# Attention with adaptive layer norm: transposing pairs of bfloat16 columns as one float32

## The chip, the core and the metric

The kernel runs on one core of a Trainium2 chip. A core has five engines that run their own instruction streams and wait for each other through semaphores: TensorE (matmuls, called PE in the profile, its weight loads PEld), VectorE (DVE), ScalarE (ACT), GpSimd (POOL) and SyncE (SP), which here only issues DMA transfers. [...] The metric is the device time of one execution in microseconds (us), lower is better.

## The reference

The program is one transformer block with conditioning. Cut to what matters:

```python
mod = (silu(c) @ w_mod).reshape(1, 6, 1, 640)          # sa, ca, ga, sb, cb, gb
h = layernorm(x) * (1 + ca) + sa                        # x: [1, 2048, 640]
q = (h @ wq) per head                                   # 32 heads, width 128
p = softmax(q @ k_cache.T * 128 ** -0.5)                # [32, 2048, 2048]
x = x + ga * ((p @ v_cache) @ wo)
h = layernorm(x) * (1 + cb) + sb
x = x + gb * B(h)                                       # token-mixing block and MLP, F = 1728
```

All inputs and the output are bfloat16. The keys and values of the 32 heads (2048 x 128 each) are inputs; the softmax runs over 2048 keys for each of 2048 queries.

## The kernel before

**Order of the work.** The kernel is written as one long list of operations; a small recorder (class `Prog`) appends each to its engine's stream in the order of the program, derives which other operations it depends on from the names of the buffers it reads (`r`) and writes (`w`), and emits semaphore waits for them. Nothing is reordered later, so the order in the code is the order on each engine. A transfer belongs to the stream of the engine that issues it; nearly all are issued by SyncE, one after the other.

**Stages.** A preamble loads x, normalizes it, transposes it into `hT` and computes the modulation rows. Then comes the attention loop (line 552), which takes most of the time, and last the output projection and block B.

**The attention loop.** One step `s` handles one tile of 128 queries of one head (`h, j = divmod(s, 16)`): 32 heads x 16 tiles = 512 steps, and 12 more to drain. In a step:

- `qk(s, half)`: TensorE computes the scores of the 128 queries against 2048 keys into the PSUM buffer `Sps`, in two halves of 1024 keys (two matmuls of 512 columns each). There is one `Sps`, so a half is free only when VectorE has read it.
- L594: VectorE reads each half, multiplies by -scale, writes it as float32 into `negS` (three buffers) and takes the minimum. L604: GpSimd combines the two halves' minima.
- L607: ScalarE computes the exponential of the 2048 columns into the bfloat16 tile `Pb` of a ring of `RP = 10` tiles.
- The tile has to be transposed so that keys lie on the partitions. This goes one of two ways. Most tiles go by DMA: `transpose(g, n)` (L231) has SyncE issue a transpose of one or two neighbouring tiles from `Pb` to `PTs`. The tiles named in `PE_STEPS` go over TensorE instead: tiles 3 and 10 of a head, and tiles 2, 3 and 10 in every fourth head (`h % 4 == 1`), 72 of 512 in all.
- `pv(g, half)` (L314), eight steps later (`PVD`): sixteen matmuls of the transposed tile, as weights, with `Vaug`, which holds V and a column of ones that yields the softmax's denominator. The result is accumulated in PSUM (`PO`), copied out by ScalarE every second step (L585), divided by GpSimd (L462) and written to DRAM (`o_scratch`).
- `q_piece` (L246) and `q_evac` (L253): the projection of the next head's queries is spread over the steps in 20 matmuls; ScalarE copies it out four times a head.

SyncE also issues, in each head, the transposing load of the next keys (L214, at j = 2), the load of wq (j = 6) and of V (j = 9).

**Transposes on TensorE.** `t_piece(g, r, q)` does a quarter of a tile: four 128x128 bfloat16 blocks, each loaded as weights and multiplied with the identity `ident` in transpose mode, into one of two PSUM banks (`JBb`, shared with the query projection). A tile takes two steps, named by the second numbers in `PE_STEPS`: r = 0 in the first, r = 1 in the second. After two pieces `t_evac(g, r)` copies 1024 bfloat16 columns from PSUM to the ring. ScalarE does it (L271, 104 times) except where `by_dve` holds (r = 1 of tiles 2 and 3), where VectorE does (L273, 40 times). In the stream, ScalarE's copies stand ahead of the step's exponential; VectorE's stand behind its two halves of the scores.

`PTs[:, b, kt, :]` is the block of key tile `kt` with the 128 queries side by side; PV reads it as weights without a step.

Of the kernel before, what the change touches and what calls it, by code (L numbers as in the profile page):

```python
# [8 lines left out]
BF16 = mybir.dt.bfloat16  # L9
# [114 lines left out]
def bass_adaLN_cond__mha_block_cached__mixer_s_mlp__prompt_kernel(  # L124
# [6 lines left out]
    KT = D // 128  # L131
# [14 lines left out]
    with ExitStack() as es:  # L146
# [3 lines left out]
        ident = sb("ident", [128, 128], BF16)  # L150
        mod_bc = sb("mod_bc", [128, 4 * D], F32)
# [6 lines left out]
        if True:  # L158
            with ExitStack() as es1:
# [6 lines left out]
                sb1("pad", [128, 32], F32)  # L166
# [4 lines left out]
                small = sb1("small", [128, 4 * NQT + 32], F32)  # L171
                hTx = sb1("hTx", [128, US], BF16)
                Of = sb1("Of", [128, 4, 2, 130], F32)
                On = sb1("On", [128, 2, 4, 128], BF16)
                mv = small[:, 0:2 * NQT].rearrange("p (t z) -> p t z", z=2)
# [12 lines left out]
                PTs = ring[:, RP:2 * RP].rearrange("p r (k q) -> p r k q", k=NKT)  # L188
                flat = ring[:].rearrange("p r s -> p (r s)")
# [16 lines left out]
                assert CO + 8 * KT <= 2 * RP * SK and XO + NQT * D <= WO_ and WO_ + KT * 2 * D <= 10 * SK  # L206
# [49 lines left out]
                def t_piece(g, r, q):  # L256
                    jb = bank(("t", g, r))

                    def f(t):
                        for z in range(4 * q, 4 * q + 4):  # L260
                            kt = 8 * r + z
                            ins = t.transpose(JBb[jb][:, z * 128:(z + 1) * 128], Pb[:, g % RP, kt * 128:(kt + 1) * 128], ident[:])
                        return ins
                    G.op("tensor", f, r=[("Pb", g % RP)], w=[("J", jb)])

                def t_evac(g, r):
                    jb = bank(("t", g, r))
                    dst = PTs[:, g % RP, r * 8:(r + 1) * 8, :]
                    src = JBb[jb].rearrange("p (k q) -> p k q", k=8)
                    if not by_dve(g, r):  # L270
                        G.op("scalar", lambda a: a.copy(dst, src), r=[("J", jb)], w=[("PT", g % RP, r)])  # L271
                    else:
                        G.op("vector", lambda v: v.tensor_copy(dst, src), r=[("J", jb)], w=[("PT", g % RP, r)])  # L273

                by_dve = lambda g, r: r == 1 and g % NQT in (2, 3)
# [31 lines left out]
                def pv(g, half):  # L307
                    hb = (g // NQT) % 2
                    b = g % RP
                    ob = PO[:, ((g // 2) % 2) * 512 + (g % 2) * 130:]  # L310

                    def f(t):
                        for kt in range(half * 8, half * 8 + 8):
                            ins = t.matmul(ob[:, 0:129], PTs[:, b, kt, :], Vaug[:, hb, kt, 0:129],  # L314
                                           start=(kt == 0), stop=(kt == NKT - 1))
                        return ins
                    G.op("tensor", f, r=[("PT", b, half), ("V", hb), "ones"], w=[("O", (g // 2) % 2)])
# [34 lines left out]
                G.op("gpsimd", lambda g: g.memset(ident[:], 0.0), w=["id0"])  # L352
                G.op("gpsimd", lambda g: g.memset(ones_f, 1.0), w=["onesf"])
                G.op("gpsimd", lambda g: g.affine_select(out=ident[:], in_=ident[:], pattern=[[-1, 128]],
                                                         compare_op=ALU.not_equal, fill=1.0, base=0, channel_multiplier=1),
                     r=["id0"], w=["ident"])
                G.op("gpsimd", lambda g: g.memset(Vaug[:, :, :, 128:130], 1.0), w=["ones"])
# [38 lines left out]
                def to_hT(cc):  # L396
                    for k in range(KT):
                        b = (4, 5, 3, 4, 5)[k % 5] if cc == NQC - 1 else (cc * KT + k) % 6

                        def f(t, k=k, b=b):  # L400
                            for z in range(4):
                                ins = t.transpose(TB[b][:, z * 128:(z + 1) * 128], x_sb[:, 4 * cc + z, k * 128:(k + 1) * 128], ident[:])
                            return ins
                        G.op("tensor", f, r=["ident"] + [("xh", 4 * cc + z) for z in range(4)] + XK[cc], w=[TK[b]])
# [147 lines left out]
                for s in range(NG + PVD + LAG):  # L552
# [35 lines left out]
                    for fn, x, y in evacs:  # L588
                        if fn is q_evac or not by_dve(x, y):
                            fn(x, y)  # L590
                    for half in range(2):
                        if s < NG:
                            r8 = s % 8
                            G.op("vector", lambda v, half=half, s=s, r8=r8: v.tensor_scalar(  # L594
                                out=negS[:, s % 3, half * 1024:(half + 1) * 1024],
                                in0=Sps[:, half * 1024:(half + 1) * 1024],
                                scalar1=-SCALE, scalar2=None, op0=ALU.mult, op1=ALU.min,
                                accum_out=(nm0 if half == 0 else nm1)[:, r8:r8 + 1]),
                                r=[("S", half)], w=[("negS", s % 3), ("nmh", half, r8)])
                    for fn, x, y in evacs:  # L600
                        if fn is t_evac and by_dve(x, y):
                            fn(x, y)
# [307 lines left out]
```

## Time and profile before

| | |
|---|---|
| Time, median of 3 runs | 1569.87 us (1567.64 to 1571.41) |
| Profiled execution, span from first to last instruction | 1568.9 us (this one has no time recorded beside its span) |
| Attention loop, first to last L594 | 35.4 to 1251.8 us |
| TensorE / VectorE / ScalarE / GpSimd busy | 1472.3 / 1398.3 / 1275.9 / 623.0 us |
| L594, VectorE, 1024 times | 1177.7 us, mean of one 1224 ns |
| L607, ScalarE, 512 times | 1045.7 us, mean of one 2066 ns |
| L262, TensorE transposes, 1152 times | 218 ns each, overlapping |
| L271 ScalarE copies, 104; L273 VectorE copies, 40 | 1.06 and 0.69 us each |
| L231, transposes by DMA, 248 issues | median 4.34 us on SyncE's queue, 7.1 us to landing |
| TensorE clock granted | 0.998 of full |

How to read the profile: a line of the groups gives the source line, the engine, the operation, output <- input, shapes and count; then busy time, mean of one, and the time its engine stood idle just ahead of it with what ended that idle time. A timeline row is start, length, engine, line and operation; `x2` means that two neighbours were merged. Lengths of neighbours on one engine overlap, so what an instruction costs its engine is the distance to the next start. In the lines of waits the three numbers are total us, times and the longest.

### The profile page before, as it was taken

The page shows a single profiled execution, that of the slowest core. Times are in us where ns is not written, and L with a number is a line of the kernel's source. Part 1 is how long each engine was busy: PE and PEld are TensorE (multiplying, and loading weights), DVE is VectorE, ACT ScalarE, POOL GpSimd, SP SyncE. Part 2 cuts the span into 40 slices and gives each one's busy share as a digit, 9 for nine tenths or more (in the row PEclk, how much of TensorE's full clock was granted, in tenths as well). Part 3 has the DMA queues.
Part 4 walks back from the last instruction along what each step waited for, and adds up shares of the span by engine and source line. Part 5 has one row for each costly group of instructions (what it writes and reads, how often), then busy time and mean ns, then how long its engine had stood idle before and what let it go on. Part 6 is the DMA issues. An engine that isn't in the chain of part 4 may idle for free.

```text
span 1568.9 us, 33553 instructions
## 1 busy us (share of the span) xinstructions
PE 1472.3 (94%) x13947; PEld 923.4 (59%) x13175; DVE 1398.3 (89%) x2471; ACT 1275.9 (81%) x1121; POOL 623.0 (40%) x1396
## 2 busy tenths in 40 slices
PE   5899999999999999999999999999999899999999
PEld 3466666666665566566656666566566655554545
DVE  6999999999999999999999999999999937667435
ACT  4999999999999999999999999999999900034230
POOL 0144444444444444444444444444444433323100
PEclk9999999999999999999999999999999999999999
DMA  9999999999999999999999999999999999725100
GB/s 298 239 221 239 237 242 237 233 241 243 237 240 233 239 232 232 240 236 235 229 237 236 233 243 249 226 242 243 235 241 237 238 246 190 157 53 144 38 22 34
DMA packets 1172828, 334.59 MB, mean 213 GB/s; under 512 B 1153280, under 2 KB 1166656, under 8 KB 1172672
## 3 DMA queue, kind: packets, MB, share of 16 engines
q1 hardware_dynamic: 1164192, 311.30, 100.8%
q0 software_dynamic: 6144, 16.79, 3.5%
q10 hardware_dynamic: 2336, 4.34, 0.8%
q8 instruction: 108, 1.77, 0.5%
q14 instruction: 48, 0.39, 0.1%
HBM read 43.48 MB, written 19.40 MB: 40 GB/s over the span
## 4 chain that ended last, share of the span: by engine, by line
ACT 40%; DVE 23%; PE 19%; DMA 9%; issue 7%; POOL 1%; POOLq 0%; DVEq 0%
ACT ring L607 32%; DVE negS L594 20%; DMA ring<-ring 8%; PE Sps L540 8%; PE Sps L847 4%; ACT ring L271 3%; ACT kv L253 2%; ACT Of L585 2%; PE QPp L798 2%; PE Oaug L798 2%; DVE ring L273 1%; PE Sps L783 1%; DVE ring L379 1%; DMA negS<-o_scratch 1%; PE PTp L314 1%
## 5 line engine op out<-in xcount | busy, mean ns | idle before, releaser
L594 DVE TENSOR_SCALAR_CACHE_REDUCE negS<-Sps 128x1024 f32<-128x1024 f32 x1024 | 1177.7, 1224 | 19.4 <-PE Sps L15 18.5
L607 ACT ACTIVATE ring<-negS,small 128x2048 bf16<-128x2048 f32 x512 | 1045.7, 2066 | 13.7 <-POOL small L604 12.5
L314 PEld LDWEIGHTS PTp<-kv,ring 128*128 128x128 bf16 x8192 | 554.1, 98 | 325.0 <-issue 69.6
L314 PE MATMUL PTp<-kv,ring 128*128 128x129 bf16 x8192 | 645.3, 220 | 25.0 <-DMA ring<-ring 23.9
L15 PE MATMUL Sps<-kv 128*128 128x512 bf16 x1024 | 387.9, 379 | 16.8 <-DVE negS L594 9.9
L604 POOL TENSOR_SCALAR small<-small 128x1 f32<-128x1 f32 x512 | 146.4, 286 | 621.8 <-DVE negS L594 621.7
L301 PE MATMUL Sps<-kv 128*128 128x512 bf16 x919 | 354.3, 386 | 27.8 <-DVE negS L594 16.5
L462 POOL TENSOR_SCALAR On<-Of,small 128x128 bf16<-128x128 f32 x512 | 191.0, 373 | 13.0
L301 PEld LDWEIGHTS Sps<-kv 128*128 128x128 bf16 x1024 | 98.1, 96 | 141.7 <-DVE negS L594 121.6
L455 POOL TENSOR_TENSOR small<-Of,small 128x4 f32<-128x4 f32 x128 | 133.1, 1040 | 8.8 <-ACT Of L585 8.7
L469 POOL DMA_DIRECT2D o_scratch<-On x128 | 103.1, 806 | 40.8 <-POOL On L462 37.2
L585 ACT COPY Of<-PTp 128x259 f32<-128x259 f32 x256 | 108.6, 424 | 13.2 <-PE PTp L314 13.2
L246 PE MATMUL Oaug<-hTx,kv 128*128 128x512 bf16 x268 | 101.9, 385 | 3.7 <-DVE hTx L411 3.7
L246 PE MATMUL QPp<-hTx,kv 128*128 128x512 bf16 x259 | 97.7, 382 | 2.6 <-ACT hTx L406 2.1
L728 ACT ACT_TABLE_LOAD x1 | 1.3, 1283 | 112.6 <-POOL hTx L746 112.6
L594 DVE DVE_READ_ACCUMULATOR negS<-Sps 128x1 f32 x1024 | 90.3, 88 | 0.0
L271 ACT COPY ring<-Oaug 128x1024 bf16<-128x1024 bf16 x72 | 77.0, 1069 | 0.0
L641 POOL TENSOR_SCALAR negS<-negS 128x1 f32<-128x1 f32 x48 | 24.2, 504 | 125.2 <-DVE negS L650 125.2
L540 PE MATMUL Sps<-wo,negS 128*128 128x128 bf16 (+1 forms) x503 | 69.9, 298 | 1.2 <-DMA negS<-o_scratch 0.8
L540 PE MATMUL Sps<-wo,hTx 128*128 128x512 bf16 (+1 forms) x502 | 69.3, 297 | 0.5
L851 DVE TENSOR_TENSOR ring<-Sps,ring 128x640 f32<-128x640 f32 x15 | 12.4, 824 | 59.5 <-PE Sps L847 59.5
L655 DVE TENSOR_TENSOR ring<-Sps,mod_bc 128x640 f32<-128x640 f32 x16 | 13.1, 821 | 53.6 <-PE Sps L540 32.9
(88 smaller groups left out, 1052.7 us busy)
## 6 DMA issues: line engine op xcount, KB each, us to landing
kv<-in_A_v_cache_dram SPq DMA_DIRECT2D x32, 512.0 KB, 5.0
o_scratch<-On POOLq DMA_DIRECT2D x128, 128.0 KB, 4.7
kv<-in_A_wq_dram SPq DMA_DIRECT2D x32, 160.0 KB, 3.2
wo<-in_A_wo_dram SPq DMA_DIRECT2D x1, 5120.0 KB, 16.5
ring<-ring SPq DMA_TRANSPOSE x248, 7.1
ring<-in_A_x_dram SPq DMA_DIRECT2D x5, 640.0 KB, 6.6
ring<-in_w_mod_dram SPq DMA_DIRECT2D x1, 3200.0 KB, 13.8
out_dram<-wo SPq DMA_DIRECT2D x15, 160.0 KB, 1.8
```

Source lines behind the costliest of these rows:

```text
L15: return t.add_instruction(mybir.InstMatmult(name=t.bass.get_next_instruction_name(), ins=[t.lower_ap(rhs), t.lower_ap(lhsT)], outs=[t.low ...
L246: G.op("tensor", lambda t: t.matmul(JB[jb], wq[:, hb, q, :], hT[:, q, cc * 512:(cc + 1) * 512], start=(q == 0), stop=(q == KT - 1)), r=[(" ...
L271: G.op("scalar", lambda a: a.copy(dst, src), r=[("J", jb)], w=[("PT", g % RP, r)])
L301: ins = (t.matmul if c2 == 0 else partial(same_weights, t))(Sps[:, col:col + 512], QT[:, hb, j * 128:(j + 1) * 128], KTs[:, hb, col:col + ...
L314: ins = t.matmul(ob[:, 0:129], PTs[:, b, kt, :], Vaug[:, hb, kt, 0:129], start=(kt == 0), stop=(kt == NKT - 1))
L455: G.op("gpsimd", lambda g: g.tensor_tensor(out=rl[:, 4 * b:4 * b + 4], in0=Of[:].rearrange("p a z d -> p (a z) d")[:, 4 * b:4 * b + 4, 128 ...
L462: G.op("gpsimd", lambda g: g.tensor_scalar(out=On[:, b, z, :], in0=Of[:, 2 * b + z // 2, z % 2, 0:128], scalar1=rl[:, 4 * b + z:4 * b + z ...
L540: ins = t.matmul(YB[b][:, c0:c0 + cw], OTj[pr % 2][:, 2 * hh + z, :], wo[:, hh, c0:c0 + cw], start=(hh == 0), stop=(hh == H - 1))
L585: G.op("scalar", lambda a, p=p: a.copy(Of[:, p % 4].rearrange("p z d -> p (z d)")[:, 0:259], PO[:, (p % 2) * 512:(p % 2) * 512 + 259]), r= ...
L594: G.op("vector", lambda v, half=half, s=s, r8=r8: v.tensor_scalar(out=negS[:, s % 3, half * 1024:(half + 1) * 1024], in0=Sps[:, half * 102 ...
L604: G.op("gpsimd", lambda g, r8=r8: g.tensor_scalar(out=nm[:, r8:r8 + 1], in0=nm0[:, r8:r8 + 1], scalar1=nm1[:, r8:r8 + 1], scalar2=None, op ...
L607: G.op("scalar", lambda a, s=s, r8=r8: a.activation(Pb[:, s % RP, :], negS[:, s % 3, :], ACT.Exp, bias=nm[:, r8:r8 + 1], scale=-1.0), r=[( ...
```

## The change

The tiles that go over TensorE are moved as float32: two neighbouring bfloat16 columns count as one 4-byte element.

- `t_piece` reads `Pb` as 1024 float32 columns and does two 128x128 float32 transposes in a quarter where there were four bfloat16 ones, with a float32 identity `identf`. The PSUM bank then holds, for each of 128 pairs and each query, the pair.
- So that a pair holds the columns i and 128 + i of a block of 256 keys, VectorE writes `negS` interleaved for these tiles (`is_pe(s)`): the output pattern runs over 128 elements with a step of two float32. The exponential passes the order on.
- `t_evac` copies 512 float32 columns, always on ScalarE; `by_dve` is gone, and the copies that were behind VectorE's halves now stand ahead of the exponential on ScalarE.
- `pv` reads the weights of such a tile from `PTr` with a step of two bfloat16.
- The ones in `Vaug` are no longer a memset: GpSimd writes pairs (1, 0) into the ring, TensorE transposes them as float32, ScalarE copies them, and GpSimd writes `Vaug`'s ones from the result. `identf` is a GpSimd copy of `ident`.
- In SBUF `ident` moves into the ring's preamble part, `mod_bc` and `small` change places, `pad` goes. Which tiles go over TensorE and which by DMA (`PE_STEPS`, `is_pe`) is the same.

```diff
-        ident = sb("ident", [128, 128], BF16)
-        mod_bc = sb("mod_bc", [128, 4 * D], F32)
...
-                sb1("pad", [128, 32], F32)
+                small = sb1("small", [128, 4 * NQT + 32], F32)
...
-                small = sb1("small", [128, 4 * NQT + 32], F32)
+                mod_bc = sb1("mod_bc", [128, 4 * D], F32)
...
+                identf = sb1("identf", [128, 128], F32)
...
+                PTr = ring[:, RP:2 * RP].rearrange("p r (k q z) -> p r k q z", k=NKT // 2, z=2)
...
                 def t_piece(g, r, q):
                     jb = bank(("t", g, r))
+                    src = Pb[:, g % RP, :].bitcast(F32)
 
                     def f(t):
-                        for z in range(4 * q, 4 * q + 4):
-                            kt = 8 * r + z
-                            ins = t.transpose(JBb[jb][:, z * 128:(z + 1) * 128], Pb[:, g % RP, kt * 128:(kt + 1) * 128], ident[:])
+                        for z in range(2 * q, 2 * q + 2):
+                            c0 = (4 * r + z) * 128
+                            ins = t.transpose(JB[jb][:, z * 128:(z + 1) * 128], src[:, c0:c0 + 128], identf[:])
                         return ins
-                    G.op("tensor", f, r=[("Pb", g % RP)], w=[("J", jb)])
+                    G.op("tensor", f, r=[("Pb", g % RP), "identf"], w=[("J", jb)])
 
                 def t_evac(g, r):
                     jb = bank(("t", g, r))
-                    dst = PTs[:, g % RP, r * 8:(r + 1) * 8, :]
-                    src = JBb[jb].rearrange("p (k q) -> p k q", k=8)
-                    if not by_dve(g, r):
-                        G.op("scalar", lambda a: a.copy(dst, src), r=[("J", jb)], w=[("PT", g % RP, r)])
-                    else:
-                        G.op("vector", lambda v: v.tensor_copy(dst, src), r=[("J", jb)], w=[("PT", g % RP, r)])
-
-                by_dve = lambda g, r: r == 1 and g % NQT in (2, 3)
+                    dst = ring[:, RP + g % RP, r * 1024:(r + 1) * 1024].bitcast(F32)
+                    G.op("scalar", lambda a: a.copy(dst, JB[jb]), r=[("J", jb)], w=[("PT", g % RP, r)])
...
-                            ins = t.matmul(ob[:, 0:129], PTs[:, b, kt, :], Vaug[:, hb, kt, 0:129],
+                            pt = PTr[:, b, kt // 2, :, kt % 2] if is_pe(g) else PTs[:, b, kt, :]
+                            ins = t.matmul(ob[:, 0:129], pt, Vaug[:, hb, kt, 0:129],
...
-                G.op("gpsimd", lambda g: g.memset(Vaug[:, :, :, 128:130], 1.0), w=["ones"])
+                G.op("gpsimd", lambda g: g.tensor_copy(identf[:], ident), r=["ident"] + ringk(IO, IO + 128), w=["identf"])
+                half1 = flat[:, 0:256].rearrange("p (q z) -> p q z", z=2)
+                G.op("gpsimd", lambda g: g.memset(half1, 0.0), w=["h0", ("Pb", 0)])
+                G.op("gpsimd", lambda g: g.memset(half1[:, :, 0], 1.0), r=["h0"], w=["h1"])
+                G.op("tensor", lambda t: t.transpose(JB[0][:, 0:128], flat[:, 0:256].bitcast(F32), identf[:]),
+                     r=["h1", "identf"], w=[("J", 0)])
+                G.op("scalar", lambda a: a.copy(flat[:, 256:512].bitcast(F32), JB[0][:, 0:128]), r=[("J", 0)], w=["h2"])
+                G.op("gpsimd", lambda g: g.tensor_copy(
+                    Vaug[:, :, :, 128:130], flat[:, 256:384].rearrange("p (b k y z) -> p b k y z", b=2, k=NKT, z=2)[:, :, :, :, 0]),
+                    r=["h2", ("Pb", 0)], w=["ones"])
...
                     for fn, x, y in evacs:
-                        if fn is q_evac or not by_dve(x, y):
-                            fn(x, y)
+                        fn(x, y)
                     for half in range(2):
                         if s < NG:
                             r8 = s % 8
-                            G.op("vector", lambda v, half=half, s=s, r8=r8: v.tensor_scalar(
-                                out=negS[:, s % 3, half * 1024:(half + 1) * 1024],
-                                in0=Sps[:, half * 1024:(half + 1) * 1024],
-                                scalar1=-SCALE, scalar2=None, op0=ALU.mult, op1=ALU.min,
+                            dst = negS[:, s % 3, half * 1024:(half + 1) * 1024]
+                            src = Sps[:, half * 1024:(half + 1) * 1024]
+                            if is_pe(s):
+                                dst = dst.rearrange("p (b i z) -> p b z i", b=4, z=2)
+                                src = src.rearrange("p (b z i) -> p b z i", b=4, z=2)
+                            G.op("vector", lambda v, half=half, dst=dst, src=src, r8=r8: v.tensor_scalar(
+                                out=dst, in0=src, scalar1=-SCALE, scalar2=None, op0=ALU.mult, op1=ALU.min,
                                 accum_out=(nm0 if half == 0 else nm1)[:, r8:r8 + 1]),
                                 r=[("S", half)], w=[("negS", s % 3), ("nmh", half, r8)])
-                    for fn, x, y in evacs:
-                        if fn is t_evac and by_dve(x, y):
-                            fn(x, y)
```

More of the change, by code (lines that the diff above doesn't have):

```diff
@@ L205, in bass_adaLN_cond__mha_block_cached__mixer_s_mlp__prompt_kernel @@
                 s_col = flat[:, CO + 7 * KT:CO + 8 * KT]
-                assert CO + 8 * KT <= 2 * RP * SK and XO + NQT * D <= WO_ and WO_ + KT * 2 * D <= 10 * SK
+                IO = CO + 8 * KT
+                ident = flat[:, IO:IO + 128]
+                assert IO + 128 <= 2 * RP * SK and XO + NQT * D <= WO_ and WO_ + KT * 2 * D <= 10 * SK
                 PO = PTp[:].bitcast(F32)
@@ L350, in bass_adaLN_cond__mha_block_cached__mixer_s_mlp__prompt_kernel @@
                 G.dma("sync", lambda e: e.dma_start(wo[:], A_wo.rearrange("(h p) n -> p h n", p=128)), "wo", w=["wo", "woz", "wo4"])
-                G.op("gpsimd", lambda g: g.memset(ident[:], 0.0), w=["id0"])
+                G.op("gpsimd", lambda g: g.memset(ident, 0.0), w=["id0"])
                 G.op("gpsimd", lambda g: g.memset(ones_f, 1.0), w=["onesf"])
-                G.op("gpsimd", lambda g: g.affine_select(out=ident[:], in_=ident[:], pattern=[[-1, 128]],
+                G.op("gpsimd", lambda g: g.affine_select(out=ident, in_=ident, pattern=[[-1, 128]],
                                                          compare_op=ALU.not_equal, fill=1.0, base=0, channel_multiplier=1),
                      r=["id0"], w=["ident"])
-                G.op("gpsimd", lambda g: g.memset(Vaug[:, :, :, 128:130], 1.0), w=["ones"])
+                G.op("gpsimd", lambda g: g.tensor_copy(identf[:], ident), r=["ident"] + ringk(IO, IO + 128), w=["identf"])
[8 more added lines that the diff above has]
+                    r=["h2", ("Pb", 0)], w=["ones"])
                 G.op("scalar", lambda a: a.activation(s_col, c_sb, ACT.Silu), r=["c"], w=["scol"])
@@ L401, in f @@
                             for z in range(4):
-                                ins = t.transpose(TB[b][:, z * 128:(z + 1) * 128], x_sb[:, 4 * cc + z, k * 128:(k + 1) * 128], ident[:])
+                                ins = t.transpose(TB[b][:, z * 128:(z + 1) * 128], x_sb[:, 4 * cc + z, k * 128:(k + 1) * 128], ident)
                             return ins
-                        G.op("tensor", f, r=["ident"] + [("xh", 4 * cc + z) for z in range(4)] + XK[cc], w=[TK[b]])
+                        G.op("tensor", f, r=["ident"] + [("xh", 4 * cc + z) for z in range(4)] + XK[cc] + ringk(IO, IO + 128), w=[TK[b]])
                         if k % 2 == 0:
```

## The prediction

> **What bounds the kernel now.** I read the page's busy shares first. TensorE 94%, VectorE 89% and ScalarE 81% leave no clear bound, so I went to the attention loop (first to last L594: 35.4 to 1251.8 us, 1216 us for 512 steps) and to its groups of instructions:
>
> ```profile
> PE 1472.3 (94%) x13947; PEld 923.4 (59%) x13175; DVE 1398.3 (89%) x2471; ACT 1275.9 (81%) x1121; POOL 623.0 (40%) x1396
> ...
> L594 DVE TENSOR_SCALAR_CACHE_REDUCE negS<-Sps 128x1024 f32<-128x1024 f32 x1024 | 1177.7, 1224 | 19.4 <-PE Sps L15 18.5
> L607 ACT ACTIVATE ring<-negS,small 128x2048 bf16<-128x2048 f32 x512 | 1045.7, 2066 | 13.7 <-POOL small L604 12.5
> ...
> L271 ACT COPY ring<-Oaug 128x1024 bf16<-128x1024 bf16 x72 | 77.0, 1069 | 0.0
> ```
>
> Both engines hardly idle. Their durations overlap their neighbours, so I took prices from start to start. VectorE's timeline, then ScalarE's (start, length):
>
> ```profile
> 247.61 1.23 DVE L594 TENSOR_SCALAR_CACHE_REDUCE negS<-Sps 128x1024 f32<-128x1024 f32 x1
> 248.75 0.09 DVE L594 DVE_READ_ACCUMULATOR negS<-Sps 128x1 f32 x1
> 248.75 0.69 DVE L273 COPY ring<-QPp 128x1024 bf16<-128x1024 bf16 x1
> 249.35 1.22 DVE L594 TENSOR_SCALAR_CACHE_REDUCE negS<-Sps 128x1024 f32<-128x1024 f32 x1
> ```
> ```profile
> 226.17 1.01 ACT L271 COPY ring<-QPp 128x1024 bf16<-128x1024 bf16 x1
> 227.06 2.02 ACT L607 ACTIVATE ring<-negS,small 128x2048 bf16<-128x2048 f32 x1
> 228.96 0.38 ACT L585 COPY Of<-PTp 128x259 f32<-128x259 f32 x1
> 229.22 3.91 ACT L607 ACTIVATE ring<-negS,small 128x2048 bf16<-128x2048 f32 x2
> ```
>
> A half of the scores takes VectorE 1.145 us, its tile copy 0.60. ScalarE: tile copy 0.89, exponential 1.90, output copy 0.26, and a query copy (L253) 0.46. VectorE's sum over the loop is 1024 x 1.145 + 40 x 0.60 = 1196.5 us, and with the 19.4 us idle that is the loop. A reader could stop here and call VectorE the bound. The next view says why not: SyncE's queue, which issues the transposes done by DMA. Its rows are start and length of an issue. A ring transpose holds the queue for 4.34 us in the median and has landed 7.1 us after its start (the page's list of issues), so the queue moves on when the transfer is most of the way; the next issue starts 0.04 us later:
>
> ```profile
> 207.26 2.40 SPq L214 DMA_TRANSPOSE kv<-in_A_k_cache_dram  x1
> 209.70 4.88 SPq L231 DMA_TRANSPOSE ring<-ring  x1
> 214.63 0.58 SPq L218 DMA_DIRECT2D kv<-in_A_wq_dram  x1
> 215.25 8.95 SPq L231 DMA_TRANSPOSE ring<-ring  x2
> 224.25 0.58 SPq L223 DMA_DIRECT2D kv<-in_A_v_cache_dram  x1
> 224.87 17.95 SPq L231 DMA_TRANSPOSE ring<-ring  x4
> 242.86 2.75 SPq L214 DMA_TRANSPOSE kv<-in_A_k_cache_dram  x1
> 245.65 4.33 SPq L231 DMA_TRANSPOSE ring<-ring  x1
> ```
>
> There is no hole in it. The transpose issued at 224.87 belongs to step 75, whose exponential ended at 217.80 + 2.16 = 219.96: it stood in line for 4.9 us. Going through all issues from 100 to 1250 us I find twelve gaps over 0.1 us, 5.8 us in sum, the longest 1.33. By head: the issues of a head with two TensorE tiles (24 "plain" heads) fill 38.2 us on average, those of every fourth head, which has three (8 of them), 35.4; by the starts of L594 the heads take 37.9 and 38.3; VectorE's work needs 32 x 1.145 + 0.60 = 37.2 and + 1.20 = 37.8. So in plain heads the queue falls behind by 1 us a head until PV waits for it, and in the fourth it catches up and has its few gaps. The waits between 50 and 1260 us show the first half:
>
> ```profile
> DVE negS L594 <- PE Sps L15: 12.5, 22, 1.4
> ...
> PE PTp L314 <- DMA ring<-ring: 23.9, 37, 1.7
> ```
>
> VectorE's stalls are TensorE's waits for DMA, one step removed. (The queue's own waits name ScalarE for 900 us; that view counts the holds as idle.)
>
> **The change part by part.**
> - VectorE loses 40 copies: 40 x 0.60 = 24 us, leaving 1172.5.
> - VectorE writes 144 halves (72 tiles) with a step of 8 bytes. No row here writes with a step. Nearest is the same instruction without it, 1.145; the far end is twice that. I take 0, since count, source and engine stay, and keep +1.145 x 144 = 165 us of VectorE time as the bad end; no gain is possible, as the element count is the same. [...]
> - ScalarE: 104 copies of 1024 columns go (104 x 0.89 = 92.6 us), 144 of 512 columns come. The row to price them is the mod_bc copy L451, also 128x512 f32 from f32: two in 1.05 us with the first 0.59, so 0.46 each: 66 us. Net -26. A plain head then costs 16 x 1.90 + 8 x 0.26 + 4 x 0.46 + 4 x 0.46 = 36.2, the fourth 37.1, both below today's 37.0 and 37.9. Bad end: 0.89 each, +36 us. The copies moved from VectorE's order into ScalarE's stand ahead of the step's exponential; they are ready 0.47 (PV) + 0.22 (transposes) + 0.46 after the second QK, while VectorE's half (1.22) and POOL's maximum (0.29) hold that exponential anyway.
> - TensorE: 1152 transposes become 576 of f32. The timeline prices what is there:
>
> ```profile
> 220.45 0.63 PE L314 MATMUL PTp<-kv,ring 128*128 128x129 bf16 x8
> 220.92 0.39 PE L262 MATMUL Oaug<-ident,ring 128*128 128x128 bf16 x4
> 221.14 0.38 PE L301 MATMUL Sps<-kv 128*128 128x512 bf16 x1
> ```
>
>  Eight PV matmuls 0.47, four transposes 0.22 (0.055 each), and QK's two 0.43. Bounds for an f32 transpose: 0.055 if the width costs nothing, 0.315 if load (0.097) and matmul (0.218) no longer overlap. I take 0.11, two of today's, because 4 bytes a column is two bfloat16: no change. Base of a head is 32 x 0.90 + 20 query matmuls x 0.215 = 33.1; with x per f32 transpose it is 33.1 + 16x plain and 33.1 + 24x in the fourth, so 34.9 and 35.7 at 0.11. [...]
> - PV of those tiles reads its weights with a step of 4 bytes (1152 loads). Between today's pace 0.059 and the load's full 0.098: +0.31 per half at worst, +1.2 us plain, +1.9 in the fourth head. I take 0; at worst 36.1 and 37.6, still under what the heads take today (37.9 and 38.3).
> - Start: five POOL instructions (0.15 to 0.3 each by the rows at 0.73 to 1.58 us), one transpose, one ScalarE copy ahead of Silu. ScalarE waits for c until 6.49 and TensorE's first work is at 12.6, so both cover it; POOL's next work is at 6.97. Without that cover it would be 2 to 3 us.
> - Moved buffers, and no DMA: issues, sizes and the set of tiles each way stay.
>
> The sum: VectorE -24, ScalarE -26, TensorE 0, SyncE's queue 0. The queue is what is late next. What can go is its idle time: 5.8 us, and in the first two heads, where it still waits for exponentials (gaps of 0.97 and 2.66 at 81 and 95 us), VectorE's lead of 0.6 + 1.2 = 1.8. About 7 us in all. 1568.9 - 7 = 1562 for the profiled span; the runs' median lies 1.0 above that span: 1563.
>
> **The rivals.**
> - B, the queue is no wall: if holds shorten once requests come earlier, all 24 us go, less new stalls of some 5: 1546 to 1555. Against it: issues have the same length whether the line is long (head 12: pairs 4.1 to 5.4) or empty (head 30: 4.1 to 5.2).
> [...]
> - D, slower: TensorE is the bound at the f32 transposes. The point is x = 0.22. At the full 0.315 a plain head is 38.1 (+0.2), the fourth 40.7 (+2.3): 24 x 0.2 + 8 x 2.3 = 24 us, 1594. For it: no f32 matmul runs in this kernel. Against: TensorE hides loads everywhere else.
> - E, the stepped write costs double: plain head 36.6 + 4 x 1.145 = 41.2, fourth 43.5; 24 x 3.3 + 8 x 5.2 = 121 us, 1691.
> - F, ScalarE's f32 copy costs 0.89: fourth head 39.7, +1.4 and no slack for the queue to catch up: 1581 to 1590.
>
> **How the numbers follow.** A (the forecast) 0.50, own range 1558 to 1567; B 0.10; C 0.16; D 0.12; E 0.08; F 0.04. What this kernel can tell from no change is about 0.2%, 3.1 us. Faster: 0.44 of A (0.06 of it lands too near) and B = 0.54. Same: 0.06 + 0.13 of C = 0.19. Slower: 0.27. For 8 in 10 I leave out E (0.08) and the outer halves of B and D (0.05 + 0.06): 1552 to 1594.
>
> **What would show it.** Right: no L273 group; the L271 copy near 550 to 600 ns; L594 still 1.145 start to start in stepped halves; the SyncE queue without gaps; VectorE idle up from 19 to about 36 us, with PE and PEld waiting longer for the ring transposes. Wrong: stepped halves longer; waits of L594 for TensorE right after f32 transposes; gaps in the queue that stay; or holds that shorten.

## The result, and the profile after

The changed kernel takes 1560.94 us in the median of four runs (1559.17 to 1562.39), the kernel before 1570.64 us in four runs beside it (1567.64 to 1574.86). The ratio is 0.9933, with a 95% interval of 0.991 to 0.9956: 9.7 us faster, some 0.7%. Four runs of the kernel before are few: in 67 more, taken beside the experiments below, its median is 1568.6 us (1564.0 to 1578.34), so the gain may be as small as 7.7 us, which the interval allows. The profiled execution took 1561.13 us with a span of 1559.0, against 1568.9 before. The attention loop went from 35.4–1251.8 to 35.7–1240.8 us, so it ends 11.0 us earlier; what follows the loop became 1.1 us longer. So the gain is all in the loop.

The page of the changed kernel, its busy line and the three groups that answer to those shown of before:

```profile
PE 1469.7 (94%) x13383; PEld 901.2 (58%) x12600; DVE 1376.7 (88%) x2431; ACT 1258.6 (81%) x1163; POOL 625.6 (40%) x1399
...
L606 DVE TENSOR_SCALAR_CACHE_REDUCE negS<-Sps 128x1024 f32<-128x1024 f32 x1024 | 1176.9, 1221 | 29.6 <-PE Sps L15 28.5
L614 ACT ACTIVATE ring<-negS,small 128x2048 bf16<-128x2048 f32 x512 | 1037.2, 2042 | 19.1 <-POOL small L611 17.5
...
L313 PE MATMUL PTp<-kv,ring 128*128 128x129 bf16 x8192 | 645.6, 220 | 41.7 <-DMA ring<-ring 40.5
```

TensorE's PV matmuls and the two lines of the scores' matmuls on the page of the kernel before:

```profile
L314 PE MATMUL PTp<-kv,ring 128*128 128x129 bf16 x8192 | 645.3, 220 | 25.0 <-DMA ring<-ring 23.9
L15 PE MATMUL Sps<-kv 128*128 128x512 bf16 x1024 | 387.9, 379 | 16.8 <-DVE negS L594 9.9
L301 PE MATMUL Sps<-kv 128*128 128x512 bf16 x919 | 354.3, 386 | 27.8 <-DVE negS L594 16.5
```

The scores' matmuls on the page of the changed kernel:

```profile
L15 PE MATMUL Sps<-kv 128*128 128x512 bf16 x1008 | 381.8, 379 | 5.9 <-DVE negS L606 2.0
L299 PE MATMUL Sps<-kv 128*128 128x512 bf16 x957 | 366.9, 383 | 16.0 <-DVE negS L606 5.4
```

TensorE, VectorE and ScalarE are all a little less busy than before, and yet VectorE idles more ahead of its main instruction (19.4 to 29.6 us), and so does ScalarE (13.7 to 19.1). VectorE got rid of 24 us of copies and 10 of them came back as idle time. On TensorE the idle time moved: ahead of PV, where it waits for DMA, it went from 25.0 to 41.7 us, and ahead of the scores from 44.6 down to 21.9, of which waits for VectorE were 26.4 and are 7.4. The waits of the changed kernel between 50 and 1260 us (total us, times, longest) name where from:

```profile
PE PTp L313 <- DMA ring<-ring: 40.5, 65, 2.1
...
DVE negS L606 <- PE Sps L15: 22.4, 40, 1.8
```

TensorE waits 65 times for a tile that a DMA transposes, and VectorE stands behind TensorE. The timeline of the queue that issues those transposes (start, length), over the same head as shown of before:

```profile
206.58 2.49 SPq L216 DMA_TRANSPOSE kv<-in_A_k_cache_dram  x1
209.12 5.37 SPq L233 DMA_TRANSPOSE ring<-ring  x1
214.53 0.58 SPq L220 DMA_DIRECT2D kv<-in_A_wq_dram  x1
215.16 8.46 SPq L233 DMA_TRANSPOSE ring<-ring  x2
223.67 0.58 SPq L225 DMA_DIRECT2D kv<-in_A_v_cache_dram  x1
224.30 17.75 SPq L233 DMA_TRANSPOSE ring<-ring  x4
242.09 2.77 SPq L216 DMA_TRANSPOSE kv<-in_A_k_cache_dram  x1
244.90 4.39 SPq L233 DMA_TRANSPOSE ring<-ring  x1
```

Each start is the end of the row above plus 0.04 to 0.06 us. Taken over all issues:

| | before | after |
|---|---|---|
| gaps over 0.1 us in SyncE's queue, 100 to 1250 us | 12, sum 6.4 us | 3, sum 1.1 us |
| the same, 60 to 100 us | 5.7 us | 2.4 us |
| all 248 ring transposes, time that they hold the queue | 1072.5 us | 1069.3 us |
| mean wait in line, from the end of the exponential to the issue | 2.46 us | 3.31 us |
| a head with two TensorE tiles ("plain"), by the starts of VectorE's halves, mean of heads 1 to 30 | 37.75 us | 37.69 us |
| a head with three ("fourth"), the same | 38.35 us | 37.18 us |

(The prediction put the first entry at 5.8; by the rule of this table it is 6.4. Its 37.9 us for a plain head has the first head in it, which takes 41.6.) The gaps shrank by 5.3 and 3.2 us and the holds by 3.2; together 11.7, which is the loop's 11.0 within 0.7. Only the gaps can be put down to the change: the same 248 issues hold the queue for 1073.6 and 1064.7 us in two other forms of the changed kernel (PV a step later, and the copies back on VectorE, both below), so 3.2 us is within what holds differ by from kernel to kernel. The last two rows show how it looks from the engines: a plain head hardly changed, the fourth head lost 1.17 us, and three plain heads and a fourth now take 37.56 us on average. The prediction had measured how long the queue's issues fill a head: 38.2 in a plain one, 35.4 in a fourth, which is 37.5 on average. Over heads 1 to 30 and with the 0.04 us between issues they fill 37.66 us on average before, where heads take 37.91, and 37.57 after, where heads take 37.56. The loop now runs at the queue's pace.

The single prices. PE's timeline of the changed kernel at a pair of the new transposes, between eight PV matmuls and the next QK:

```profile
126.48 0.63 PE L313 MATMUL PTp<-kv,ring 128*128 128x129 bf16 x8
126.95 0.39 PE L265 MATMUL Oaug<-identf,ring 128*128 128x128 f32 x2
127.19 0.39 PE L299 MATMUL Sps<-kv 128*128 128x512 bf16 x1
```

And the groups of these transposes by shape, the matmuls and their weight loads (busy us, mean ns of one):

```profile
L265 PE MATMUL Oaug<-identf,ring 128*128 128x128 f32 x288 | 55.5, 274 | 0.0
...
L265 PEld LDWEIGHTS Oaug<-identf,ring 128*128 128x128 f32 x288 | 29.6, 142 | 0.4
```

Two float32 transposes take 0.24 us to the next start here, some 0.12 each, where four bfloat16 ones took 0.22 in the prediction's rows; over all of them the median is 0.23 us in both kernels. One lasts longer on record (274 ns against 218, its load 142 against 97), but lengths overlap. VectorE's timeline, where the first and the last row are ordinary halves and the two between are the interleaved halves of a TensorE tile (step 35; rows of the accumulator's read-out left out):

```profile
119.04 1.22 DVE L606 TENSOR_SCALAR_CACHE_REDUCE negS<-Sps 128x1024 f32<-128x1024 f32 x1
...
120.18 1.22 DVE L606 TENSOR_SCALAR_CACHE_REDUCE negS<-Sps 128x1024 f32<-128x1024 f32 x1
...
121.33 1.22 DVE L606 TENSOR_SCALAR_CACHE_REDUCE negS<-Sps 128x1024 f32<-128x1024 f32 x1
...
122.47 1.22 DVE L606 TENSOR_SCALAR_CACHE_REDUCE negS<-Sps 128x1024 f32<-128x1024 f32 x1
```

All four are 1.14 to 1.15 us apart; over all 144 interleaved halves the median is 1.144, over the others 1.145. And ScalarE's timeline with two of the new copies:

```profile
129.99 0.70 ACT L272 COPY ring<-Oaug 128x512 f32<-128x512 f32 x1
130.45 2.13 ACT L614 ACTIVATE ring<-negS,small 128x2048 bf16<-128x2048 f32 x1
132.36 0.49 ACT L593 COPY Of<-PTp 128x259 f32<-128x259 f32 x1
132.61 0.72 ACT L272 COPY ring<-QPp 128x512 f32<-128x512 f32 x1
133.09 4.04 ACT L614 ACTIVATE ring<-negS,small 128x2048 bf16<-128x2048 f32 x2
```

From start to next start a copy costs 0.46 to 0.48 us, the exponential still 1.9.

### The profile page after: what moved, and what is told of

Same layout as the page of the kernel before. It is cut to its first block, busy times and chain, and to the rows that moved or that the text cites. A ratio compares the mean times of both kernels' runs of the same rounds, so it can differ in the third digit from the quotient of the medians.

```text
span 1559.0 us, 32417 instructions
## 1 busy us (share of the span) xinstructions
PE 1469.7 (94%) x13383; PEld 901.2 (58%) x12600; DVE 1376.7 (88%) x2431; ACT 1258.6 (81%) x1163; POOL 625.6 (40%) x1399
## 4 chain that ended last, share of the span: by engine, by line
ACT 43%; PE 19%; DVE 16%; DMA 14%; issue 5%; POOL 2%; SPq 0%; POOLq 0%; DVEq 0%
ACT ring L614 35%; DVE negS L606 15%; DMA ring<-ring 12%; PE Sps L548 7%; PE Sps L854 4%; ACT ring L272 3%; ACT Of L593 2%; ACT kv L255 2%; PE Oaug L805 2%; PE QPp L805 2%; DMA negS<-o_scratch 1%; PE PTp L313 1%; PE Sps L790 1%; POOL o_scratch L477 1%; POOL small L611 1%
## 5 line engine op out<-in xcount | busy, mean ns | idle before, releaser
L606 DVE TENSOR_SCALAR_CACHE_REDUCE negS<-Sps 128x1024 f32<-128x1024 f32 x1024 | 1176.9, 1221 | 29.6 <-PE Sps L15 28.5
L614 ACT ACTIVATE ring<-negS,small 128x2048 bf16<-128x2048 f32 x512 | 1037.2, 2042 | 19.1 <-POOL small L611 17.5
L313 PE MATMUL PTp<-kv,ring 128*128 128x129 bf16 x8192 | 645.6, 220 | 41.7 <-DMA ring<-ring 40.5
L593 ACT COPY Of<-PTp 128x259 f32<-128x259 f32 x256 | 102.1, 399 | 15.2 <-PE PTp L313 15.2
L248 PE MATMUL Oaug<-hTx,kv 128*128 128x512 bf16 x257 | 97.8, 385 | 3.7 <-DVE hTx L419 3.7
L606 DVE DVE_READ_ACCUMULATOR negS<-Sps 128x1 f32 x1024 | 86.2, 84 | 0.0
L858 DVE TENSOR_TENSOR ring<-Sps,ring 128x640 f32<-128x640 f32 x15 | 12.4, 824 | 59.5 <-PE Sps L854 59.5
L548 PEld LDWEIGHTS Sps<-wo,negS 128*128 128x128 bf16 x512 | 40.0, 98 | 33.0 <-DMA negS<-o_scratch 1.1
```

The source lines that it names most:

```text
L248: G.op("tensor", lambda t: t.matmul(JB[jb], wq[:, hb, q, :], hT[:, q, cc * 512:(cc + 1) * 512], start=(q == 0), stop=(q == KT - 1)), r=[(" ...
L313: ins = t.matmul(ob[:, 0:129], pt, Vaug[:, hb, kt, 0:129], start=(kt == 0), stop=(kt == NKT - 1))
L548: ins = t.matmul(YB[b][:, c0:c0 + cw], OTj[pr % 2][:, 2 * hh + z, :], wo[:, hh, c0:c0 + cw], start=(hh == 0), stop=(hh == H - 1))
L593: G.op("scalar", lambda a, p=p: a.copy(Of[:, p % 4].rearrange("p z d -> p (z d)")[:, 0:259], PO[:, (p % 2) * 512:(p % 2) * 512 + 259]), r= ...
L606: G.op("vector", lambda v, half=half, dst=dst, src=src, r8=r8: v.tensor_scalar(out=dst, in0=src, scalar1=-SCALE, scalar2=None, op0=ALU.mul ...
L614: G.op("scalar", lambda a, s=s, r8=r8: a.activation(Pb[:, s % RP, :], negS[:, s % 3, :], ACT.Exp, bias=nm[:, r8:r8 + 1], scale=-1.0), r=[( ...
```

## Is the queue the wall? Its load taken away

The theory is that SyncE's queue, with the transfers behind it, sets the loop's pace, so that 24 us less on VectorE and 26 less on ScalarE are worth only what idle time the queue had left. Then the same change must be worth all of VectorE's 24 us where the queue has time to spare. The rival is that the gain is small for a reason in the engines (an operation that costs more, a new stall). Both kernels were run without the key loads from the third head on. Those heads compute with old keys, so 30 holds of some 2.4 us and their transfers are gone, and nothing else.

```diff
-                        if j == 2 and h >= 1 and h + 1 < H:
+                        if j == 2 and h < 0:
```

The kernel before, so relieved:

> The kernel before, without the key loads of heads 2 to 31 (those heads use the keys already in SBUF, so the output is another). It takes some 2.4 us a head off SyncE's queue and 0.5 MB off the DMA engines. Theory Q (the queue of DMA transposes is the wall in plain heads): the queue needs about 35.7 us in a plain head, less than VectorE's 37.2, so the loop falls to the work of VectorE and ScalarE, 1196 us and some 8 of start: 13 to 16 us less than before, 1554 to 1558 us, no more PE waits for ring transposes. Rival V (the engines are the wall, the queue only looks full): no change, 1570.

1555.09 us in the median (1553.5 to 1557.16), ratio 0.991 (0.9885 to 0.9935), as expected. The heads take 37.22 and 37.82 us, which is VectorE's work in them (37.24 and 37.84 from 1.145 and 0.60). The page of this kernel, VectorE's group:

```profile
L594 DVE TENSOR_SCALAR_CACHE_REDUCE negS<-Sps 128x1024 f32<-128x1024 f32 x1024 | 1176.7, 1259 | 6.3 <-PE Sps L15 6.0
```

Of those 6.3 us, the waits between 50 and 1260 us hold 0.2: inside the loop VectorE never stops. With a lighter queue the kernel before is bound by VectorE; as it was, it was not. The changed kernel, relieved in the same way:

> The changed kernel, without the key loads of heads 2 to 31, as in the kernel before. Theory Q: the loop falls to VectorE's 1172.5 us and some 10 of start and stalls, 20 to 25 us under the changed kernel's 1561: 1536 to 1541; so with the queue relieved the change is worth 16 to 22 us, twice and more of the 9.7 that it gave. Rival V: the change is worth the same 10 us with or without the queue.

1531.07 us (1530.85 to 1531.7), ratio 0.9754 (0.973 to 0.9778), below the range expected, because no stall was left: the heads take 36.65 and 36.63 us, VectorE's 32 halves. The change is worth 1555.09 − 1531.07 = 24.0 us here, and 7.7 to 9.7 us with the key loads. The 40 copies of 0.60 us are 24 us; that it agrees so closely is luck, since the single runs allow 22 to 26. Its queue (start, length) now has holes, 75 us of them in sum between 100 and 1250 us:

```profile
207.05 0.58 SPq L220 DMA_DIRECT2D kv<-in_A_wq_dram  x1
207.96 8.99 SPq L233 DMA_TRANSPOSE ring<-ring  x2
...
244.01 0.59 SPq L220 DMA_DIRECT2D kv<-in_A_wq_dram  x1
244.97 9.03 SPq L233 DMA_TRANSPOSE ring<-ring  x2
```

0.33 and 0.37 us lie between the end of an issue and the next start, where the changed kernel as it is has 0.04 to 0.06. The theory holds: nothing in the new operations eats the gain. What these two runs do not separate is the issuing queue from the DMA engines that do its transfers, since a load that is left out relieves both. The page's row of the DMA engines reads 9 (90% or more) in every slice of the loop in all four kernels, so it does not tell them apart either. "The queue" below means both.

## Would waiting longer for the transposes help?

If TensorE's waits for DMA were a matter of latency (a tile that arrives a little late), using each tile one step later would end them. If they are a matter of rate, a later use only lengthens the line. The changed kernel with PV nine steps behind instead of eight (V's load in each head moves with it by one step):

```diff
-                PVD = 8
+                PVD = 9
```

> The changed kernel with PV nine steps behind the scores instead of eight: a transposed tile has 2.3 us longer to arrive. Theory Q (the queue's throughput is the wall): its sum of holds is the same, so 1557 to 1562. Rival L (it is only the latency of one transfer that stalls PV, so a longer lead removes the 22 us of VectorE's stalls): 1538 to 1545.

1560.12 us (1559.76 to 1561.77), ratio 0.9951 (0.9939 to 0.9964): as without the edit, within the intervals, and not the 1538 to 1545 of the rival. VectorE's group on the page of this kernel:

```profile
L606 DVE TENSOR_SCALAR_CACHE_REDUCE negS<-Sps 128x1024 f32<-128x1024 f32 x1024 | 1175.6, 1222 | 31.5 <-PE Sps L15 30.9
```

And its waits for the ring between 50 and 1260 us:

```profile
PE PTp L313 <- DMA ring<-ring: 36.7, 45, 2.6
```

The waits are fewer (45 for 65) but as long in sum (36.7 for 40.5 us); the mean wait in line grew from 3.31 to 5.25 us, and the queue's gaps are 1.1 us as before the edit. It is a rate.

## Which part of the change brings the gain?

The change does two things for the engines: VectorE loses its copies, ScalarE's copies get shorter. First the changed kernel with the 40 copies put back on VectorE, now as float32:

```diff
-                    G.op("scalar", lambda a: a.copy(dst, JB[jb]), r=[("J", jb)], w=[("PT", g % RP, r)])
+                    if not by_dve(g, r):
+                        G.op("scalar", lambda a: a.copy(dst, JB[jb]), r=[("J", jb)], w=[("PT", g % RP, r)])
+                    else:
+                        G.op("vector", lambda v: v.tensor_copy(dst, JB[jb]), r=[("J", jb)], w=[("PT", g % RP, r)])
+
+                by_dve = lambda g, r: r == 1 and g % NQT in (2, 3)
```

> The changed kernel with the 40 copies (r = 1 of tiles 2 and 3) back on VectorE behind its halves, now of 512 float32 columns, some 0.6 us each as before. ScalarE is lighter than in either kernel (104 x 0.46). Theory Q: VectorE needs 37.2 and 37.8 us again, so the fourth heads take 37.8 and the queue idles there again: the gain goes, 1566 to 1571. Rival S (the gain came from ScalarE's 26 us): it stays or grows, 1555 to 1561.

1563.26 us in the median of eleven runs (1557.43 to 1565.65), ratio 0.9962 (0.9946 to 0.9979): between the two ranges that were expected, with about half of the gain left by the two ratios. The groups by shape of this kernel show what the copies cost there:

```profile
L273 ACT COPY ring<-Oaug 128x512 f32<-128x512 f32 x72 | 42.6, 592 | 0.0
...
L275 DVE COPY ring<-QPp 128x512 f32<-128x512 f32 x40 | 27.4, 685 | 0.0
```

On VectorE a copy of 512 float32 lasts 685 ns; one of 1024 bfloat16 lasted 690 (the L273 group of before, 27.6 us for 40). From start to next start both take 0.60 us. Packing gained VectorE nothing per copy. The heads are at 37.37 (plain) and 38.02 us (fourth), so the fourth head is again near VectorE's own work.

Then each engine's relief alone, in the kernel before. In the first of two, ScalarE's copies write half of the columns (the other half is left out), so ScalarE is about 45 us lighter and VectorE unchanged:

```diff
-                        G.op("scalar", lambda a: a.copy(dst, src), r=[("J", jb)], w=[("PT", g % RP, r)])
+                        G.op("scalar", lambda a: a.copy(dst[:, 0:4], src[:, 0:4]), r=[("J", jb)], w=[("PT", g % RP, r)])
```

> The kernel before with ScalarE's 104 copies cut to the first 512 of 1024 columns (the other half of those tiles is left uncopied, so the output is another). ScalarE is 104 x 0.43 = 45 us lighter, as in the run with the copies back on VectorE; VectorE, TensorE's bfloat16 transposes, buffers and queue are those of before. Theory Q by rates alone: VectorE still needs 37.8 in the fourth heads, so 1566 to 1570. Theory L (ScalarE's lag behind VectorE, 1.07 us in the mean before, eats the lead that PV has on the queue): the 5 us of that earlier run come back, 1561 to 1565. If neither, and it stays at 1569 while the earlier run was 1563, those 5 us came from the float32 form or the buffers.

1565.05 us in twelve runs (1561.92 to 1571.99), ratio 0.9977 (0.9963 to 0.9992): 3.7 us less than the 1568.79 beside it, at the upper end of theory L's range and below theory Q's, so the rates alone do not account for it. In the second, VectorE's 40 copies are left out, and ScalarE is unchanged:

```diff
-                        if fn is t_evac and by_dve(x, y):
+                        if fn is t_evac and by_dve(x, y) and x < 0:
```

> The kernel before with VectorE's 40 copies left out (their halves of the tiles stay uncopied, so the output is another). VectorE is 24 us lighter, ScalarE as before: 37.0 us in a plain head, 37.9 in the fourth. Theory Q by rates: plain heads stay with the queue, the fourth go from VectorE's 37.8 to ScalarE's 37.9, so next to nothing is gained: 1565 to 1570. If VectorE's load alone is what counts: 1561.

1565.01 us in twelve runs (1561.83 to 1572.32), ratio 0.9978 (0.9964 to 0.9992): 3.8 us less, at the lower end of what was expected, although VectorE has the whole 24 us less to do. VectorE's group on the page of the kernel with ScalarE relieved:

```profile
L594 DVE TENSOR_SCALAR_CACHE_REDUCE negS<-Sps 128x1024 f32<-128x1024 f32 x1024 | 1176.6, 1222 | 14.0 <-PE Sps L15 13.7
```

And on the page of the one with VectorE relieved:

```profile
L594 DVE TENSOR_SCALAR_CACHE_REDUCE negS<-Sps 128x1024 f32<-128x1024 f32 x1024 | 1177.3, 1220 | 32.2 <-PE Sps L15 27.6
```

With VectorE's copies gone its idle time went from 19.4 to 32.2 us: half of what it was spared it spends waiting. With ScalarE relieved VectorE idles less, 14.0. The two reliefs act in different heads: VectorE's takes the fourth head to 37.01 us and leaves the plain one at 37.82; ScalarE's takes the plain head to 37.45 and leaves the fourth at 38.40. Each alone is worth 3.7 to 3.8 us, about half of what the change gains. They are not its two halves: here ScalarE is spared 45 us, in the change 26, and no run has both reliefs in the kernel before. That ScalarE's part works through an earlier exponential is argued, not shown: the mean time from the end of VectorE's second half to the start of the exponential fell from 1.06 to 0.59 us in that run, but no run moved that time alone.

The opposite test puts the 40 copies on ScalarE without making them shorter, in the kernel before:

```diff
-                by_dve = lambda g, r: r == 1 and g % NQT in (2, 3)
+                by_dve = lambda g, r: False
```

> The kernel before with all 144 copies of 1024 bfloat16 columns on ScalarE, none on VectorE: the other half of the change alone. By the prices of before ScalarE then needs 37.9 us in a plain head and 39.7 in the fourth. Theory Q with ScalarE as the next wall: the fourth heads go from 38.3 to 39.7 or more and the queue idles in them: 1578 to 1586. Rival: taking the copies off VectorE is what counts, 1561.

1589.6 us (1586.74 to 1590.95), ratio 1.0124 (1.0101 to 1.0148): slower, by some 4 us more than expected. The waits of this kernel between 50 and 1260 us:

```profile
DVE negS L594 <- ACT ring L607: 24.5, 62, 0.6
```

And its ScalarE timeline:

```profile
247.62 1.53 ACT L271 COPY ring<-QPp 128x1024 bf16<-128x1024 bf16 x1
248.51 2.54 ACT L607 ACTIVATE ring<-negS,small 128x2048 bf16<-128x2048 f32 x1
250.41 0.90 ACT L585 COPY Of<-PTp 128x259 f32<-128x259 f32 x1
```

A copy costs 0.89 us here, and VectorE waits 62 times for ScalarE to free a buffer of `negS`. ScalarE has become the bound in every head: 38.0 us in plain heads and 39.8 in the fourth make 24 x 38.0 + 8 x 39.8 = 1230 us, and the loop took 1233; by the starts of its exponentials the heads take 38.06 and 39.75, and between 50 us and the loop's end ScalarE idles 0.2 us. The expectation had the fourth heads so, and the plain ones not. So the move off VectorE was possible only with the shorter copy: without the packing it costs some 20 us, with it, it gains.

## What do the float32 transposes cost TensorE?

The prediction took 0.11 us for one and gave 0.22 as the price from which TensorE is the bound. The changed kernel with each of them done twice has that price by construction:

```diff
-                            ins = t.transpose(JB[jb][:, z * 128:(z + 1) * 128], src[:, c0:c0 + 128], identf[:])
+                            for _ in range(2):
+                                ins = t.transpose(JB[jb][:, z * 128:(z + 1) * 128], src[:, c0:c0 + 128], identf[:])
```

> The changed kernel with each float32 transpose issued twice into the same place. At the measured 0.115 us it adds 576 x 0.115 = 66 us of TensorE work, all in the steps that transpose. Theory Q with cover on TensorE: a plain head then needs 33.1 + 16 x 0.23 = 36.8 us of TensorE (hidden under 37.7), the fourth 38.6 against 37.2 today: 8 x 1.4 = 11 us, 1568 to 1574. Rival T (TensorE is already on the path in those steps): all 66 us, 1627. Rival 0 (it hides wholly): 1561.

1568.44 us (1565.82 to 1573.12), ratio 1.0001 (0.9985 to 1.0016): the whole gain is gone, inside the range expected. TensorE's timeline of this kernel:

```profile
204.71 0.60 PE L266 MATMUL Oaug<-identf,ring 128*128 128x128 f32 x4
205.15 0.38 PE L300 MATMUL Sps<-kv 128*128 128x512 bf16 x1
```

And VectorE's from a microsecond later on:

```profile
205.94 1.22 DVE L607 TENSOR_SCALAR_CACHE_REDUCE negS<-Sps 128x1024 f32<-128x1024 f32 x1
...
207.12 1.23 DVE L607 TENSOR_SCALAR_CACHE_REDUCE negS<-Sps 128x1024 f32<-128x1024 f32 x1
...
208.46 1.23 DVE L607 TENSOR_SCALAR_CACHE_REDUCE negS<-Sps 128x1024 f32<-128x1024 f32 x1
...
209.80 1.23 DVE L607 TENSOR_SCALAR_CACHE_REDUCE negS<-Sps 128x1024 f32<-128x1024 f32 x1
```

Four take 0.44 us, 0.11 each, so the price holds in a stream of four as well. In the steps that transpose, the last two distances above are 1.34 us instead of 1.145, as are 158 of them in the whole loop: TensorE's 0.47 + 0.44 + 0.43 for a half. TensorE's waits for the ring fell to 0.9 us and the queue has 25 us of gaps, so in these steps TensorE is the bound, and the queue no longer is. One price, 0.22, does not show where the threshold lies.

## Moving the split

If the queue is the wall and both engines now have time left, more tiles should go over TensorE. The number of heads with three TensorE tiles is one line, `kind`. Every second head instead of every fourth (80 tiles instead of 72, 240 issues instead of 248), in the changed kernel and in the kernel before:

```diff
-                kind = lambda h: 1 if h % 4 == 1 else 0
+                kind = lambda h: 1 if h % 2 == 1 else 0
```

> The changed kernel with three TensorE tiles in every second head instead of every fourth (kind 1 where h % 2 is 1): eight more tiles go over TensorE and off the queue. Theory Q: the queue needs (38.0 + 35.4) / 2 = 36.7 us a head, VectorE 36.6, ScalarE (36.2 + 37.1) / 2 = 36.7; all three nearly even, so a loop of 32 x 36.9 and the start, 1536 to 1545. Rival: the queue is not what limits it, 1561 or slower for the added TensorE and ScalarE work.

> The same in the kernel before. VectorE needs (37.2 + 37.8) / 2 = 37.5 us a head, ScalarE (37.0 + 37.9) / 2 = 37.5, the queue 36.7. Theory Q: the engines are the wall, 32 x 37.6 and the start: 1560 to 1566, so the change is worth some 22 us here instead of 10.

The changed kernel: 1545.64 us (1542.98 to 1548.66), ratio 0.9858 (0.9842 to 0.9873), 0.6 us above the range expected. The kernel before: 1565.34 us (1563.87 to 1567.36), ratio 0.9981 (0.9972 to 0.9991), as expected. At this split the change is worth 19.7 us, at least twice as much as at its own. The kernel before gains little because its engines are now the limit: the head with three tiles takes 38.07 us there against VectorE's 37.84, and the queue has 21 us of gaps.

Two heads in three (85 tiles), and all heads (96), in the changed kernel:

```diff
-                kind = lambda h: 1 if h % 4 == 1 else 0
+                kind = lambda h: 0 if h % 3 == 0 else 1
```

> The changed kernel with three TensorE tiles in two of three heads. Queue (38.0 + 2 x 35.4) / 3 = 36.3 us a head, VectorE 36.6, ScalarE (36.2 + 2 x 37.1) / 3 = 36.8. The queue is out of the way and ScalarE the wall by little: 32 x 36.9 and the start, 1538 to 1547, about the 1546 of every second head. If the queue were still the wall: 1535 or less.

```diff
-                kind = lambda h: 1 if h % 4 == 1 else 0
+                kind = lambda h: 1
```

> The changed kernel with three TensorE tiles in every head. Queue 35.4 us a head, VectorE 36.6, ScalarE 37.1, TensorE 33.1 + 24 x 0.115 = 35.9. Theory: with the queue out of the way ScalarE is the wall, 32 x 37.1 and the start, a loop of 1195 to 1200 us: 1546 to 1552, so the best split lies at two of three heads (1541). If the queue were still the wall: below 1541.

1540.78 us (1539.71 to 1543.25), ratio 0.9822 (0.9806 to 0.9838), and 1548.16 us (1547.92 to 1548.52), ratio 0.9876 (0.986 to 0.9893); both as expected. Two heads in three is the best of the kernels run with the whole computation, faster than both; against the change as it was made it is 17 us by the two ratios and 20 by the medians. The pages of the two show why it turns. Two heads in three:

```profile
L606 DVE TENSOR_SCALAR_CACHE_REDUCE negS<-Sps 128x1024 f32<-128x1024 f32 x1024 | 1175.1, 1226 | 14.0 <-PE Sps L15 12.6
L614 ACT ACTIVATE ring<-negS,small 128x2048 bf16<-128x2048 f32 x512 | 1136.9, 2481 | 2.8 <-POOL small L611 2.5
```

And all heads:

```profile
L614 ACT ACTIVATE ring<-negS,small 128x2048 bf16<-128x2048 f32 x512 | 1175.7, 3049 | 2.0 <-POOL small L611 2.0
```

At two in three VectorE idles 14.0 us, and ScalarE ahead of its exponentials 2.8; TensorE's waits for the ring are down from 40.5 to 12.4 us and the queue has 26 us of gaps. Its heads take 36.98 us on average against VectorE's 36.6 and ScalarE's 36.8 by the prices, so ScalarE is close to being the limit already. With all heads ScalarE is the wall: the median head takes 37.31 us (by the prices 37.1), the queue has 57 us of gaps, and TensorE waits 0.7 us for the ring.

## Why the prediction was right

It gave 1563 us as the likeliest, with 1558 to 1567 as that case's own range; 1560.94 was measured, and the runs bear out the mechanism it named. Point by point:

- **What bounds the kernel.** Right. The queue's pace, 37.5 us a head, is what the loop now runs at (37.56), and with the queue relieved the change is worth the 24 us that VectorE was spared.
- **The sum, 7 us.** Its terms, 5.8 and 1.8, make 7.6. The profiled span fell by 9.9, the median by 7.7 to 9.7 depending on which runs of the kernel before it is held against, so the runs do not show that the total was too small. Its terms were not all of the right size. The idle time inside 100 to 1250 us was put at 5.8 and gave back 5.3. The first heads were put at 1.8, by VectorE's lead alone, and gave back 3.2 between 60 and 100 us. The ring's holds were held constant and became 3.2 us shorter in sum, which is within what they differ by from kernel to kernel. Against these stand 1.1 us after the loop and 0.7 that these items do not close. The 1.0 us added from span to time compared the median with the span of another execution: beside their own spans the times lie 1.8 us higher before and 2.1 to 2.2 after.
- **ScalarE's 26 us.** Counted as off the path, since ScalarE's sum in a head was below VectorE's. A relief of ScalarE alone, of 45 us, is worth 3.7 us (half-size copies in the kernel before), in the plain heads, so it was not off the path. The sum came out right nevertheless because it was made at the queue, where it did not matter which engine's relief filled its gaps.
- **VectorE's interleaved write, taken as 0.** Right: 1.144 us from start to start against 1.145, so the step of 8 bytes costs nothing in this trace.
- **The float32 transpose, taken as 0.11 us.** Right: some 0.12 in a pair, 0.11 in four. The trace records 142 ns for its weight load. The transposes still follow each other every 0.11 to 0.12 us, less than that load's record, so loads overlap their neighbours.
- **ScalarE's float32 copy, taken as 0.46 us.** Right: 0.46 to 0.48. The prediction of 550 to 600 ns for its recorded length was low (617 to 625), which cost nothing.
- **PV's stepped weights, taken as 0.** Right: eight PV matmuls on a TensorE tile take 0.47 us, as the ones by DMA do.
- **The start.** Right that it is hidden: the attention loop begins 0.3 us later than before.
- **VectorE's idle time, forecast 36 us.** It is 29.6. With 24 us of copies gone and 11.0 us of loop gone, 13 us would have to come back as idle time; the page shows 10.2 more. The forecast took 7 us off the loop and so left more.
- **The rivals.** The change is not slower: the stepped write (E), the slow float32 copy (F) and the dear float32 transposes (D) fell by the prices above. C, with 0.16 of the chances, was that TensorE takes the gain back; no run of the change shows a float32 transpose that dear: it takes some 0.12 us in a pair and 0.11 in four, and the gain went only where each was done twice, 0.22 for the two. Of B, which has the holds shorten, a little may be true. The argument against it was that a hold is as long in a full line as in an empty one. Between runs that is off by some 3%: a pair holds the queue for 4.59 and 4.60 us where the mean wait in line is 2.46 and 3.31 us (before, after), and for 4.41 and 4.43 us where it is 0.76 and 0.88 (the two runs without key loads). Within one run it holds: the length of a pair's hold and its wait in line go together with a correlation of 0.01 before and -0.17 after, and with key loads and a mean wait of only 0.54 us (three TensorE tiles in all heads) a pair still takes 4.50. So the shorter holds may come from the absent key loads as well as from the shorter line; what causes them was not isolated.

## What to carry to other kernels

Before adding up what engines are spared, look for the stream that has no gaps, and look at the queues that issue transfers too: an engine that is 89% busy, with 19 us idle ahead of its main instruction, was not the only bound here: 24 us off it alone were worth 3.8, and the whole change 7.7 to 9.7 until the queue was relieved, then 24. After such a change the split of the work wants to be set again: the same change was worth 19.7 us with one line of the split altered, and the best split found was 17 to 20 us below the kernel as changed. Price each moved operation on its own engine from start to start, since the same packing halved a copy on one engine (0.89 to 0.46 us) and did nothing on another (0.60 both).

## What the runs showed of the hardware

- **A copy's price follows different things on two engines.** For the same 2 KB a partition out of PSUM, ScalarE takes 0.89 us as 1024 bfloat16 and 0.46 as 512 float32 (start to start). VectorE takes 0.60 us either way.
- **Two bfloat16 columns moved as one float32 cost TensorE what two cost.** Four bfloat16 transposes took 0.22 us to the next start in the row shown and two float32 ones 0.24; the median over all of them is 0.23 for both.
- **ScalarE's recorded length drifts while its pace does not.** The exponential's mean record is 2042 ns in the changed kernel, 2481 with two heads in three and 3049 with all heads on the three-tile split, where ScalarE hardly idles; from start to start its median is 1.91 us in all three, and 1.90 in the row above (248.51 to 250.41, with 2.54 on record). A record that grows is here a sign of an engine without slack, not of a dearer instruction.
